# A decode block on one core: one 160 KB block of Down's weights loaded in the middle of the kernel by sixteen small loads instead of near the end by one

## The chip, the cores and the metric

The kernel runs on one core of a Trainium2 chip. The metric is the device time of one execution in microseconds (us). It was run three times for the table below, and one more execution was recorded by the profiler.

## What is computed

One token passes through an attention block over a cached context and then through a gated feed-forward block. Cut to what matters:

```python
mod = (silu(c) @ w_mod).reshape(1, 6, 1, 640)          # shifts, scales, gates
h = layernorm(x) * (1 + ca) + sa
q = h @ wq                                             # 32 heads of 128
p = softmax(q @ k_cache.T * 128**-0.5)                 # 16384 positions per head
x = x + ga * ((p @ v_cache) @ wo)
h = layernorm(x) * (1 + cb) + sb
x = x + gb * ((silu(h @ w_gate) * (h @ w_up)) @ w_down)   # 640 -> 1728 -> 640
```

All tensors are bf16. The K and V caches are 134 MB each, so nearly all of the 290 MB that is read is cache. `w_down` (called Down here) has 1728 rows of 640 values, 1280 bytes a row.

## The kernel before, in words

**Pairs of heads.** The 32 heads are taken in 16 pairs, p = 0 to 15. For each pair the kernel loads 8 MB of K (`load_k`, L487) and 8 MB of V (`load_v`, L493), each as 128 rows of 64 KB, one row per SBUF partition. K goes into one of two slots of the tile `kring`, V into the single tile `vbuf`; only the last V goes into a `kring` slot. VectorE multiplies K by q in place and folds the products in halves (L543, L548, L553; for the first and the last pair L559 and L565). TensorE finishes the sums (L533, L573), the maximum and the exponentials follow (L578 to L590), and TensorE multiplies the weights with V (`pv`, L499). The order of one round is `load_k(p + 1)`, `step(p)`, `load_v(p)` (L610 to L616).

**Who may start when.** The instructions are listed by hand and sent to the engines in that order; each waits for the operations that it names. All large loads are issued by SyncE (SP) on one queue, in program order. A K load waits until the sums of the pair that had its slot are done (L488); a V load waits until `pv` of the pair before is done (L494). TensorE, VectorE and ScalarE run the middle pairs in hardware loops; SP's list is written out in full.

**The end.** After the last K there follow on SP's queue, in this order: the last V, two pieces of `wo` (L628), gate and up weights (L638 and L640), and Down in five pieces (L642 to L648): three blocks of 512 rows with four rows per partition (640 KB each), one block of 128 rows with one row per partition (rows 1536 to 1663, 160 KB), and the last 64 rows cut in halves (80 KB). The five pieces are the entries of `DOWN` (L225). The weights go into the other `kring` slot and so wait for the last pair's sums (L637).

**Down's matmuls.** L743 to L757 walk through `DOWN` in the same order. A block with four rows per partition is 16 matmuls, the block with one row per partition is 4, the last piece is 4. Each block waits for its own load. After the first block a small matmul and a VectorE step (L759, L761) prepare the last piece. L763 and L764 then scale and add, and two small stores write the 640 results.

Of the kernel before, what the change touches and what calls it, by code (L numbers as in the profile page):

```python
# [6 lines left out]
BF16 = mybir.dt.bfloat16  # L7
# [30 lines left out]
class _Plan:  # L38
# [38 lines left out]
    def op(self, eng, fn, deps=(), name="", chan=None):  # L77
        o = _Op(eng, fn, list(deps), name, len(self.ops), self.loop.get(eng), chan)
        o.sig = chan is not None
        self.ops.append(o)  # L80
        return o

    def dma(self, out_ap, in_ap, key, deps=(), name="", eng="sp", noncontig=False):
        nc = self.nc

        def fn(e, out_ap=out_ap, in_ap=in_ap, noncontig=noncontig):
            if noncontig:
                with nc.allow_non_contiguous_dma(reason="tiny vector layout change"):
                    return e.dma_start(out_ap, in_ap)
            return e.dma_start(out_ap, in_ap)  # L90

        return self.op(eng, fn, deps, name, chan=self.dma_chan(key))
# [116 lines left out]
def build(nc, A_x, A_k, A_v, A_wq, A_wo, B_wg, B_wu, B_wd, c_in, w_mod, out):  # L209
    H, S, Dh = A_k.shape[1], A_k.shape[2], A_k.shape[3]  # L210
    D = A_x.shape[2]
# [3 lines left out]
    NP = H // 2  # L215
# [6 lines left out]

    BLOCKS = [(0, 4, 0), (512, 4, 4), (1024, 4, 8), (1536, 1, 12)]

    DOWN = [(0, 0, 4), (1, 0, 4), (2, 0, 4), (3, 0, 1), (None, 0, 0)]  # L225
    FCH = NF + 1
    QW = 32
    QR = 16
    RW = D // 4
# [3 lines left out]
    with es:  # L233
        plan = _Plan(nc, es)
        op, dma = plan.op, plan.dma
        POOL, ACT, DVE, PE = "pool", "act", "dve", "pe"

        def sb(name, shape, dtype):
            return es.enter_context(nc.sbuf_tensor(name, list(shape), dtype))
# [12 lines left out]
        wd_v = kb[:, wd0:wd0 + NF * D].rearrange("p (k n) -> p k n", k=NF)  # L252
# [47 lines left out]
        rg = sb("rg", [128, FCH], F32)  # L300
        sg = sb("sg", [128, FCH], F32)
        gu_col = sb("gu_col", [128, FCH], BF16)
        gu_half = sb("gu_half", [128, 2], BF16)
        even = sb("even", [128, 2], F32)
        twice = sb("twice", [128, 64, 2], BF16)
# [114 lines left out]
        def wide(col):  # L420
            return col.broadcast_to([col.shape[0], 32])
# [38 lines left out]
        for g in range(H // 4):  # L460
            b = g % 2
# [25 lines left out]
        def load_k(p):  # L487
            deps = [o_R[p - 2]] if p >= 2 else ([o_mod[1]] if p == 1 else [])  # L488
            cuts = KCUT if p == 0 else [0, T2]
            d_k[p] = [dma(kring[:, p % 2, a:b], k_src(p)[:, a:b], ("k", p % 2, c), deps=deps, name="dma_k%d_%d" % (p, c))  # L490
                      for c, (a, b) in enumerate(zip(cuts, cuts[1:]))]

        def load_v(p):  # L493
            deps = [o_R[NP - 2]] if p == NP - 1 else [o_pv[p - 1]] if p >= 1 else [o_q[-1]]  # L494
            cuts = VCUT if p == NP - 1 else [0, T2]
            d_v[p] = [dma(v_at(p)[:, a:b, :], v_src(p)[:, a:b, :], ("v", p == NP - 1, c), deps=deps, name="dma_v%d_%d" % (p, c))
                      for c, (a, b) in enumerate(zip(cuts, cuts[1:]))]
# [100 lines left out]
        def step(p):  # L598
            reduce_mm(p, 0, score(p, 0, before(p)))
            pv(p - 1)  # L600
            o_R[p] = reduce_mm(p, 1, score(p, 1))
            diag(p - 1)
# [7 lines left out]
        for p in range(1, NP - 1):  # L610
            plan.in_loop(("pe",), "pairs", p - 1, NLOOP)
            if p >= FIRST:
                plan.in_loop(("act", "dve"), "pairs", (p - FIRST) // 2, (NP - 1 - FIRST) // 2)
            load_k(p + 1)
            step(p)
            load_v(p)  # L616
        plan.out_of_loop(("pe", "act", "dve"))


# [20 lines left out]
        d_wu = dma(wu_v, wu_src, "wu", deps=wdeps, name="dma_wu")  # L640
        d_wd = []
        for i, (b, r0, r1) in enumerate(DOWN):  # L642
            if b is None:
                dst, src = wt_v, B_wd[NF * 128:F, :].rearrange("q (h n) -> (q h) n", h=2)
            else:
                f0, n, j0 = BLOCKS[b]
                dst, src = wd_v[:, j0 + r0:j0 + r1, :], B_wd[f0:f0 + 128 * n, :].rearrange("(p r) n -> p r n", r=n)[:, r0:r1, :]
            d_wd.append(dma(dst, src, ("wd", i), deps=wdeps, name="dma_wd%d" % i))  # L648
# [93 lines left out]
        o_gum = op(DVE, lambda e: e.tensor_tensor(out=gu_col[:], in0=u_ps[:, 0:FCH], in1=sg[:], op=ALU.mult), deps=[o_sg, o_u], name="gu")  # L742
        for i, (b, r0, r1) in enumerate(DOWN):  # L743

            if b is None:
                work = [(gu_half[:, r // 2:r // 2 + 1], wt_v[:, RW * (r % 2):RW * (r % 2) + RW], r) for r in range(4)]
            else:
                j0 = BLOCKS[b][2]
                work = [(gu_col[:, j:j + 1], wd_v[:, j, RW * r:RW * r + RW], r) for j in range(j0 + r0, j0 + r1) for r in range(4)]

            def f_down(e, i=i, work=work):
                last = None
                for at, (col, rows, r) in enumerate(work):
                    last = e.matmul(f_ps[32 * r:32 * r + 32, 0:RW], lhsT=wide(col), rhs=rows, start=(i == 0 and at < 4),  # L754
                                    stop=(i == len(DOWN) - 1 and at >= len(work) - 4), tile_position=(0, 32 * r))
                return last
            prev = op(PE, f_down, deps=[o_gum if b is not None else o_guh, d_wd[i], o_nb[PL]], name="down%d" % i)  # L757
            if i == 0:
                o_tw = op(PE, lambda e: e.matmul(attn_ps[:, 8:9], lhsT=twice[64:128].rearrange("p q h -> p (q h)"), rhs=gu_col[64:128, NF:FCH], start=True, stop=True),  # L759
                          deps=[o_gum, o_twice, o_abf], name="twice_gu")  # L760
                o_guh = op(DVE, lambda e: e.tensor_tensor(out=gu_half[:], in0=attn_ps[:, 8:9].broadcast_to([128, 2]), in1=even[:], op=ALU.mult),  # L761
                           deps=[o_tw, o_even], name="gu_half")
# [10 lines left out]
def bass_adaLN_cond__gqa_block_cached__swiglu_ffn__decode_kernel(  # L773
    nc: bass.Bass,
    A_x: bass.AP,
    A_k_cache: bass.AP,
    A_v_cache: bass.AP,
    A_wq: bass.AP,
    A_wo: bass.AP,
    B_x: bass.AP,  # L780
    B_w_gate: bass.AP,
    B_w_up: bass.AP,
    B_w_down: bass.AP,
    c: bass.AP,
    w_mod: bass.AP,
    out: bass.AP,
):
    build(nc, A_x, A_k_cache, A_v_cache, A_wq, A_wo, B_w_gate, B_w_up, B_w_down, c, w_mod, out)
# [28 lines left out]
```

## Time and profile before

| what | value |
|---|---|
| time, median of 3 runs (lowest to highest) | 679.35 us (679.03 to 679.57) |
| profiled execution, its own time | 679.08 us |
| profiled execution, its span on the core | 677.8 us |
| mean granted TensorE clock | 0.590 |
| read from memory | 290.47 MB, 429 GB/s over the span |

The profiler's span runs from the first to the last instruction on the core; the execution's own time holds 1.28 us more around it. A load has three moments in the profile: its issue on SP, the time its packets take on the 16 DMA engines, and its landing, when all of its parts have counted up the semaphore. A load waits in its queue behind the loads issued before it, so the time from issue to landing is mostly time in line.

### The profile page before, as it was taken

The page shows a single profiled execution, that of the slowest core. Times are in us where ns is not written, and L with a number is a line of the kernel's source. Part 1 is how long each engine was busy: PE and PEld are TensorE (multiplying, and loading weights), DVE is VectorE, ACT ScalarE, POOL GpSimd, SP SyncE. Part 2 cuts the span into 40 slices and gives each one's busy share as a digit, 9 for nine tenths or more (in the row PEclk, how much of TensorE's full clock was granted, in tenths as well). Part 3 has the DMA queues.
Part 4 walks back from the last instruction along what each step waited for, and adds up shares of the span by engine and source line. Part 5 has one row for each costly group of instructions (what it writes and reads, how often), then busy time and mean ns, then how long its engine had stood idle before and what let it go on. Part 6 is the DMA issues. An engine that isn't in the chain of part 4 may idle for free.

```text
span 677.8 us, 5368 instructions
## 1 busy us (share of the span) xinstructions
PE 365.1 (54%) x2052; PEld 143.7 (21%) x2053; DVE 513.6 (76%) x186; ACT 46.4 (7%) x146; POOL 0.7 (0%) x6
## 2 busy tenths in 40 slices
PE   2510475755728274654818375572818465481677
PEld 1100122221312122221302122121212222130236
DVE  2189997959596896959597795959699695959812
ACT  1110000100000000000000000000000000000010
POOL 0000000000000000000000000000000000000000
PEclk9765565655657565565757555575756556575665
DMA  9999999999999999999999999999999999999997
GB/s 375 441 461 433 433 433 430 433 430 433 433 430 433 433 433 433 433 433 433 433 433 433 433 433 433 433 433 433 433 433 437 433 433 437 433 433 433 433 400 312
DMA packets 6355, 290.58 MB, mean 429 GB/s; under 512 B 714, under 2 KB 972, under 8 KB 1484
## 3 DMA queue, kind: packets, MB, share of 16 engines
q1 hardware_dynamic: 6340, 290.48, 99.3%
q8 instruction: 5, 0.08, 0.0%
q14 instruction: 2, 0.02, 0.0%
q10 hardware_dynamic: 8, 0.00, 0.0%
HBM read 290.47 MB, written 0.00 MB: 429 GB/s over the span
## 4 chain that ended last, share of the span: by engine, by line
DMA 45%; DVE 30%; issue 13%; PE 11%; ACT 0%; DVEq 0%; SPq 0%
DMA kring<-in_A_k_cache_dram 45%; DVE kring L543 10%; PE psb L533 7%; DVE kring L548 6%; DVE kring L559 5%; DVE kring L565 5%; DVE kring L553 3%; PE psb L507 1%; PE psb L712 1%; PE psb L675 1%; PE psb L573 1%; PE psb L687 0%; PE psb L754 0%; DVE pm L578 0%; DVE nb L586 0%
## 5 line engine op out<-in xcount | busy, mean ns | idle before, releaser
L543 DVE TENSOR_TENSOR kring<-kring,qbc 128x16384 bf16<-128x16384 bf16 x28 | 243.3, 8688 | 96.3 <-DMA kring<-in_A_k_cache_dram 96.3
L533 PE MATMUL psb<-kring,ident 128*128 x448 | 197.5, 607 | 119.0 <-DVE kring L553 119.0
L548 DVE TENSOR_TENSOR kring<-kring 128x8192 bf16<-128x8192 bf16 x28 | 123.8, 4420 | 0.5
L533 PEld LDWEIGHTS psb<-kring,ident 128*128 128x128 bf16 x448 | 53.8, 120 | 246.9 <-issue 246.0
L507 PE MATMUL psb<-vbuf,PZ 128*8 128x512 bf16 x960 | 83.1, 521 | 0.0
L582 PE MATMUL psb<-d,bd_f 128*128 128x64 f32 x32 | 11.0, 446 | 118.7 <-ACT d L580 118.7
L553 DVE TENSOR_TENSOR kring<-kring 128x4096 bf16<-128x4096 bf16 x28 | 64.0, 2287 | 0.5
L559 DVE TENSOR_TENSOR kring<-kring,qbc 128x16384 bf16<-128x16384 bf16 x4 | 34.8, 8688 | 23.4 <-DMA kring<-in_A_k_cache_dram 23.4
L507 PEld LDWEIGHTS psb<-vbuf,PZ 128*8 128x8 bf16 x960 | 26.3, 109 | 61.3 <-issue 52.8
L573 PE MATMUL psb<-kring,ident 128*128 128x128 bf16 (+1 forms) x48 | 14.3, 464 | 45.3 <-DVE kring L565 45.3
L582 PEld LDWEIGHTS psb<-d,bd_f 128*128 128x128 f32 x32 | 8.0, 312 | 121.2 <-DVE pm L578 111.6
L565 DVE TENSOR_TENSOR kring<-kring 128x8192 bf16<-128x8192 bf16 (+2 forms) x12 | 31.7, 2645 | 0.3
L522 PEld LDWEIGHTS psb<-sel,acc_sb 128*128 128x128 f32 x128 | 28.5, 310 | 8.4 <-issue 4.3
L522 PE MATMUL psb<-sel,acc_sb 128*128 128x2 f32 x128 | 25.6, 322 | 1.4 <-ACT acc_sb L513 1.4
L513 ACT ACTIVATE acc_sb<-psb 128x512 f32<-128x512 f32 x16 | 9.6, 597 | 212.8 <-PE psb L507 212.8
L590 ACT ACTIVATE PZ<-psb,nb 64x256 bf16<-64x256 f32 x32 | 15.0, 468 | 64.8 <-DVE nb L586 64.6
L573 PEld LDWEIGHTS psb<-kring,ident 128*128 128x128 bf16 x48 | 5.6, 122 | 52.9 <-DVE kring L565 46.1
L580 ACT ACTIVATE d<-negid,pm 128x64 f32<-128x64 f32 x16 | 5.6, 348 | 155.3 <-DVE pm L578 155.3
L466 PE MATMUL psb<-vbuf,h_col 128*128 128x512 bf16 x39 | 9.8, 415 | 8.3 <-DMA vbuf<-in_A_wq_dram 8.3
L526 ACT ACTIVATE OT_sb<-psb 128x2 f32 (+1 forms) x16 | 2.8, 172 | 150.9 <-PE psb L522 150.9
L578 DVE TENSOR_REDUCE pm<-psb 128x1 f32<-128x256 f32 x16 | 6.7, 418 | 3.7 <-PE psb L573 3.7
L466 PEld LDWEIGHTS psb<-vbuf,h_col 128*128 128x128 bf16 x40 | 3.9, 106 | 14.5 <-DMA vbuf<-in_A_wq_dram 8.8
(105 smaller groups left out, 81.1 us busy)
## 6 DMA issues: line engine op xcount, KB each, us to landing
kring<-in_A_k_cache_dram SPq DMA_DIRECT2D x2, 4096.0 KB, 40.1
vbuf<-in_A_wq_dram SPq DMA_DIRECT2D x1, 5120.0 KB, 25.6
kring<-in_w_mod_dram SPq DMA_DIRECT2D x1, 4800.0 KB, 14.0
vbuf<-in_A_wo_dram SPq DMA_DIRECT2D x1, 4480.0 KB, 22.8
kring<-in_B_w_gate_dram SPq DMA_DIRECT2D x1, 2160.0 KB, 18.7
kring<-in_B_w_up_dram SPq DMA_DIRECT2D x1, 2160.0 KB, 23.5
kring<-in_B_w_down_dram SPq DMA_DIRECT2D x3, 640.0 KB, 25.1
vbuf<-in_A_wo_dram SPq DMA_DIRECT2D x1, 640.0 KB, 24.0
```

The source lines that it names most:

```text
L466: last = e.matmul(q_ps[b][:, 0:512], lhsT=h_col[:, k:k + 1].broadcast_to([128, 128]), rhs=wq_v[:, k, g * 512:(g + 1) * 512], start=(k == 0 ...
L507: last = e.matmul(acc_ps[32 * s:32 * s + 8, :], lhsT=PZ[:, j, :], rhs=v_at(p)[:, 4 * j:4 * j + 4, :].rearrange("p t d -> p (t d)"), start= ...
L522: last = e.matmul(OT_ps[:, 0:2], lhsT=acc_sb[:, 128 * i:128 * (i + 1)], rhs=sel[:, i:8:4], start=(i == 0), stop=(i == 3))
L533: last = e.matmul(S_ps[:, 0:T2], lhsT=ident[:], rhs=kring[:, bass.ds(plan.slot(p), 1), :, d].rearrange("p o t -> p (o t)"), start=(d == 0) ...
L543: return e.tensor_tensor(out=kv4, in0=kv4, in1=q4, op=ALU.mult)
L548: o_f = op(DVE, lambda e: e.tensor_tensor(out=kv4[:, :, 0], in0=kv4[:, :, 0], in1=kv4[:, :, 1], op=ALU.add), deps=[o_m], name="fold%d_%d" ...
L553: return op(DVE, lambda e: e.tensor_tensor(out=lo[:, :, 0:QR], in0=lo[:, :, 0:QR], in1=lo[:, :, QR:QW], op=ALU.add), deps=[o_f], name="fol ...
L559: o = op(DVE, lambda e: e.tensor_tensor(out=kv, in0=kv, in1=qbc[:, p, :].unsqueeze(1).broadcast_to([128, KCUT[c + 1] - KCUT[c], 128]), op= ...
L565: o = op(DVE, lambda e, w=w: e.tensor_tensor(out=kv[:, :, 0:w], in0=kv[:, :, 0:w], in1=kv[:, :, w:2 * w], op=ALU.add), deps=[o], name="fol ...
L573: last = e.matmul(S_ps[:, a:b], lhsT=ident[:], rhs=kring[:, p % 2, a:b, d], start=(d == 0), stop=(d == 15))
L582: o_mx[p] = op(PE, lambda e: e.matmul(mx_ps[:, 0:64], lhsT=bd_f[:], rhs=d2[:], start=True, stop=True), deps=[o_d2, o_bd1, o_bd2, o_nb[p - ...
L590: o_exp[p] = op(ACT, lambda e, half=half, ps=ps: e.activation(out=PZ[ps, :, 4 * half:4 * half + 4], in_=S_ps[ps, 0:T2].rearrange("p (c i) ...
```

## The change

The block with one row per partition gets a tile of its own, `wt`. Its load is cut into sixteen loads of 15, 14, 13, 12, 11, 10, 9, 8, 8, 7, 6, 5, 4, 3, 2 and 1 rows. They are issued by SP in round p = 8, after `load_v(8)` and before `load_k(10)`, without a wait, and count on one semaphore. The load of this block at the end is gone. Its four matmuls now stand second in Down's order, between the first and the second block of four rows per partition, and read `wt`. The other engines' lists have the same instructions as before, apart from this place in TensorE's.

```diff
-    DOWN = [(0, 0, 4), (1, 0, 4), (2, 0, 4), (3, 0, 1), (None, 0, 0)]
+    DOWN = [(0, 0, 4), (3, 0, 1), (1, 0, 4), (2, 0, 4), (None, 0, 0)]
+    EARLY = [15, 14, 13, 12, 11, 10, 9, 8, 8, 7, 6, 5, 4, 3, 2, 1]
...
+        wt = sb("wt", [128, D], BF16)
         gu_half = sb("gu_half", [128, 2], BF16)
...
             step(p)
             load_v(p)
+            if p == NP // 2:
+                at = 0
+                for n in EARLY:
+                    d_wt = dma(wt[at:at + n, :], B_wd[12 * 128 + at:12 * 128 + at + n, :], "wt", name="dma_wt%d" % at)
+                    at += n
+                assert at == 128
...
         for i, (b, r0, r1) in enumerate(DOWN):
+            if b == 3:
+                d_wd.append(d_wt)
+                continue
             if b is None:
...
-                work = [(gu_col[:, j:j + 1], wd_v[:, j, RW * r:RW * r + RW], r) for j in range(j0 + r0, j0 + r1) for r in range(4)]
+                work = [(gu_col[:, j:j + 1], (wt if b == 3 else wd_v[:, j])[:, RW * r:RW * r + RW], r) for j in range(j0 + r0, j0 + r1) for r in range(4)]
```

## The prediction

> **What bounds the kernel now.** I read the page's slices first, then the chain of waits, then the end of the kernel in the timeline. The page:
>
> ```profile
> span 677.8 us, 5368 instructions
> DMA  9999999999999999999999999999999999999997
> GB/s 375 441 461 433 433 433 430 433 430 433 433 430 433 433 433 433 433 433 433 433 433 433 433 433 433 433 433 433 433 433 437 433 433 437 433 433 433 433 400 312
> DMA 45%; DVE 30%; issue 13%; PE 11%; ACT 0%; DVEq 0%; SPq 0%
> ```
>
> The 16 DMA engines are busy in every slice and move 430 to 437 GB/s from the fourth slice to the 38th. Only the last slice is not full. The queue never runs dry, so whatever is put into it in the middle pushes everything behind it back. VectorE, next on the chain, does wait in the middle; this row is from the list of VectorE's waits between 100 and 610 us:
>
> ```profile
> DVE kring L543 <- DMA kring<-in_A_k_cache_dram: 96.3, 13, 8.3
> ```
>
> It waited for K in all 13 pairs there. So up to the last K's landing the DMA stream sets the time. What follows is told by the chain from there on (start, length, what):
>
> ```profile
> 569.99 38.73 DMA kring<-in_A_k_cache_dram
> 608.75 8.69 DVE kring L559
> ...
> 673.29 0.18 DVE gu_col L742
> 673.52 0.73 PE psb L754 x16
> 674.25 0.12 PE psb L759
> 674.36 1.49 PE psb L754 x22
> 675.87 0.34 DVE qbc L763
> 676.23 0.24 DVE o_row L764
> ```
>
> From 608.75 us to the end no DMA stands on the chain: 69 us of engine work follow on one another. The time is therefore the landing of the last K plus this engine work, as long as every later load comes before it is wanted. The last ones are close. Here are Down's last three pieces: their issues, two to a row (so 648.40, 648.88 and, 0.475 us on, 649.35), and their times to landing, and then TensorE's work on them:
>
> ```profile
> 648.40 0.91 SPq L90 DMA_DIRECT2D kring<-in_B_w_down_dram  x2
> 648.88 0.91 SPq L90 DMA_DIRECT2D kring<-in_B_w_down_dram  x2
> ```
>
> ```profile
> kring<-in_B_w_down_dram SPq DMA_DIRECT2D x1, 640.0 KB, 26.2
> kring<-in_B_w_down_dram SPq DMA_DIRECT2D x1, 160.0 KB, 26.2
> ...
> kring<-in_B_w_down_dram SPq DMA_DIRECT2D x1, 80.0 KB, 25.9
> ```
>
> ```profile
> 674.29 1.39 PE L754 MATMUL psb<-kring,gu_col 128*32 128x160 bf16 x36
> 675.34 0.15 PEld L754 LDWEIGHTS psb<-kring,gu_half 128*32 128x32 bf16 x4
> 675.47 0.35 PE L754 MATMUL psb<-kring,gu_half 128*32 128x160 bf16 x4
> ```
>
> Issue plus time to landing gives 674.60 us for the third 640 KB block, 675.08 for the 160 KB block and 675.25 for the 80 KB piece. The 36 matmuls are nine groups of four; with 0.35 us for the last, 1.39 us makes eight steps of 0.13. The third block's group (the fifth) starts at 674.81 with its weights loading one step before, at 674.68; the 160 KB block's (the ninth) weights load at 675.20; the last piece's at 675.34. Each load lands some 0.1 us ahead, and the steps run on into the last piece without a hole. The end of the DMA stream and the end of the engine work meet, but TensorE waits for none of the three.
>
> **The change, part by part.**
>
> *What goes at the end.* The 160 KB load leaves the queue's end. Between 674.60 and 675.08 it took 0.48 us there. The 80 KB piece lands 0.48 us earlier against the rest. As TensorE does not wait for it, that is worth nothing here: 0, and at most 0.48 us (0.07%) if in the timed executions the loads come some tenths later than in this one. I take 0.
>
> *TensorE's order.* The four matmuls move one block ahead. Their number stays; the blocks behind them are wanted one step of 0.13 us later, so the third block's margin grows from 0.08 to 0.21 us. The wait for the 160 KB block becomes a wait for a load of 280 us before: nothing waits. 0.
>
> *SP's queue.* The sixteen issues stand between V of pair 8 and K of pair 10. The timeline of SP, and their times to landing:
>
> ```profile
> 366.31 0.33 SPq L90 DMA_DIRECT2D vbuf<-in_A_v_cache_dram  x1
> 376.35 0.33 SPq L90 DMA_DIRECT2D kring<-in_A_k_cache_dram  x1
> ```
>
> ```profile
> vbuf<-in_A_v_cache_dram SPq DMA_DIRECT2D x1, 29.6
> kring<-in_A_k_cache_dram SPq DMA_DIRECT2D x1, 38.9
> ```
>
> Issues in a row start 0.475 us apart at the end of the kernel (648.40 to 648.88), so sixteen take 7.6 us and end at 374.3. SP then waits as before for the sums of pair 8, until 376.35: 2.1 us are left. If an issue were twice as dear, K of pair 10 would be issued at 381.8, while V of pair 8 keeps the engines busy until 366.31 + 29.6 = 395.9. The cover is 14 us even then. 0.
>
> *The sixteen loads' own time.* This is the term that counts. They carry 128 rows of 1280 bytes. As one load, 128 rows are 8 on each of 16 engines and took 0.48 us with their completions: 0.06 us a row. A lone row's cost in mid-stream shows in the load of x, in a window of 0.1 us, and the whole of ScalarE's queue on the page:
>
> ```profile
> q10 hardware_dynamic: 1, 0.00, 3.4%
> ```
>
> ```profile
> q10 hardware_dynamic: 8, 0.00, 0.0%
> ```
>
> 3.4% of 16 engines in 0.1 us is 0.054 us for its one packet. The queue's eight packets are two loads of one row and a store of two rows with one completion per row: a load of n rows, n under 16, uses n engines. So an engine gets between 0 and 16 of the rows, one per load that it takes part in, and is pushed back by 0 to 16 × 0.06 = 0.96 us; on average by 0.48.
>
> [...] No view here names a DMA engine.
>
> *Which engine matters.* K counts as landed when its slowest engine is done, and the sixteen are not abreast. The windows at the end, when nothing more is queued, and the page's count of code loads:
>
> ```profile
> 673.00:673.40 0.40, 0.18 (x6) 0.10 (x4) 0.11 (x1) 0.00 (x0) 0.00 (x0) 0.50 1.07 364
> 673.40:674.00 0.60, 0.48 (x16) 0.41 (x16) 0.06 (x1) 0.00 (x0) 0.00 (x0) 0.50 0.40 150
> 674.00:674.40 0.40, 0.40 (x15) 0.21 (x9) 0.00 (x1) 0.00 (x0) 0.00 (x0) 0.50 0.28 98
> 674.40:675.30 0.90, 0.90 (x32) 0.90 (x32) 0.16 (x1) 0.00 (x0) 0.00 (x0) 0.50 0.07 23
> ```
>
> ```profile
> q8 instruction: 5, 0.08, 0.0%
> ```
>
> The DMA share (the last column but one) falls from 1.07 through 0.40 and 0.28 to 0.07: from 673.4 us on the engines drop out one after another, the last at 675.25, a spread of some 1.8 us. Packets of code, 16 KB each and put into single engines' streams, are one cause that the page shows. An engine that is ahead by a microsecond can carry up to 16 rows for nothing; the slowest pays 0.06 us for each row it gets. If it gets none, the price is 0. If it gets 16, 0.96. Nothing in the profile says which engine is slowest, so I take the middle, 8 rows and 0.48 us. The engines behind it by a few tenths can take over as the slowest, which keeps the price off 0. This delay reaches the end whole: the last K lands 0.48 us later and 69 us of engine work start from it.
>
> **Sum.** Against the profiled execution: 677.8 span + 0.48 = 678.3, and with the 1.28 us around it 679.6 (now 679.08). The three runs' median is 0.27 us above the profiled execution, so 679.8 us, 0.07% slower. Bounds of this case: 679.35 + 0 and 679.35 + 0.96, or 679.3 to 680.3. A measurement of this kernel tells some 0.2%, 1.4 us, from no change, and the whole case lies within that.
>
> **The rivals.**
>
> *Rival 1, slower: each small load holds its engine until its row has been written and counted.* Then the price of a row isn't 0.06 us. The last wait of the kernel bounds it from above:
>
> ```profile
> SPq L768 <- DMA out_dram<-o_row: 1.0, 1, 1.0
> ```
>
> A lone small store took 1.0 us from issue to landing, with all its latencies. A nearer bound is the 80 KB piece, eight rows and one completion per engine, that landed 0.17 us after the load before it. At 0.17 us per small load, an engine that takes part in all sixteen is pushed back 2.7 us and one that takes part in eight 1.4. The slowest engine decides: from eight loads on it the kernel is slower by over 0.2%, up to 682.1. Against it: eight rows of data are in those 0.17 us, so the completion alone must be less. [...] I give this rival 0.11.
>
> *Rival 2, slower: SP is stopped by the number of loads in the queue.* With K of pair 9 and V of pair 8 ahead, the sixteenth is the 18th load under way. Before, the most shows at the end:
>
> ```profile
> 635.22 0.80 SPq L90 DMA_DIRECT2D vbuf<-in_A_wo_dram  x2
> 646.92 2.86 SPq L90 DMA_DIRECT2D kring<-in_B_w_down_dram  x5
> ```
>
> ```profile
> vbuf<-in_A_wo_dram SPq DMA_DIRECT2D x1, 4480.0 KB, 22.8
> ```
>
> wo lands at 658.0, so nine loads (two of wo, gate, up, five of Down) were under way at 649.35, and the last four issues kept their pace. If there is a limit between 9 and 17, SP stands until V of pair 8 has landed at 395.9, issues the rest (up to 9 × 0.475 us) and only then K of pair 10, with idle DMA engines and up to the lone store's 1.0 us before data flow. That is 1.0 to 5.3 us, 680.4 to 684.7. Nothing in the profile speaks for such a limit. 0.05.
>
> *Rival 3, a small gain: the end of the DMA stream counts after all.* If the timed executions have TensorE waiting for the last two pieces, and the slowest engine gets few rows, the time falls by up to 0.48 us, to 678.9. The margins of 0.1 us speak for it, the even pace of the matmuls against it. 0.12. A gain of over 0.2% would need 1.4 us, and no wait of that size hangs on the block.
>
> *The forecast case* has the remaining 0.72.
>
> **How the numbers follow.** Forecast 679.8. The range starts at rival 3's end, 678.9, and ends at 681.0, which takes in the forecast case with the runs' own scatter of 0.3 us and the lower half of rival 1; rival 2 and the rest of rival 1 stay out, about 0.1. Slower by over 0.2%: nearly all of rival 2 (0.05) and two thirds of rival 1 (0.08), 0.13. Faster by over 0.2%: 0.03 for what I don't see. Within 0.2%: 0.84.
>
> **What would show it.** Right: the chain of the profile after is the same and the last K's landing (608.75) moves to 608.8 to 609.7, with the engine work behind it again 69 us; K of pair 10 is still issued when pair 8's sums are done; the sixteen issues take some 7.6 us; the DMA slices stay full in mid-kernel; the 80 KB piece lands some 0.5 us further ahead of its matmuls. Rival 1: the K behind the small loads lands over 1.4 us later than 415.2 and the delay stays. Rival 2: a SP issue of several us near 370 and a slice of lower DMA share near 396. Rival 3: a last K no later, and a shorter end. What would make the forecast wrong is a slowest engine that gets no rows, or code packets that fall on other engines than before: the spread of 1.8 us comes from where they fall, and the change lengthens SP's code by 15 loads.

## The result, and the profile after

| | before | after |
|---|---|---|
| median (lowest to highest), 20 runs each | 679.23 us (679.01 to 679.57) | 680.63 us (680.15 to 680.85) |
| ratio, 95% interval | | 1.0019 [1.0013, 1.0025] |
| profiled execution: own time, span | 679.08, 677.8 us | 680.65, 679.4 us |
| mean granted TensorE clock | 0.590 | 0.595 |

The kernel is 1.40 us slower, 0.2%. The forecast was 0.5 us. The page of the kernel after:

```profile
span 679.4 us, 5383 instructions
GB/s 379 436 460 432 432 432 429 432 429 436 432 433 432 432 432 432 432 436 432 432 432 436 432 411 432 436 436 432 432 432 432 436 432 432 432 436 432 432 408 301
DMA 49%; DVE 30%; issue 13%; PE 8%; SPq 0%; DVEq 0%
```

One slice in mid-kernel stands out: the 24th, from 391 to 408 us, moved 411 GB/s where its neighbours have 432. Before, no slice from the fourth to the 38th was under 430. The sixteen loads fall into that slice. 21 GB/s over 17 us are 0.36 MB, or 0.8 us of the stream. The page counts the small rows among what the slice moved, so most of this loss is not the moving of their bytes.

The chain of waits of the kernel after (start, length, what), from the last K on:

```profile
571.86 38.73 DMA kring<-in_A_k_cache_dram
610.62 8.69 DVE kring L561
...
650.44 26.03 DMA kring<-in_B_w_down_dram
676.51 0.89 PE psb L765 x18
677.42 0.34 DVE qbc L774
677.78 0.24 DVE o_row L775
```

The last K is in use at 610.62 instead of 608.75: 1.87 us later. At the end the chain has a new link. TensorE waits for Down's third 640 KB block, which lands at 676.47 (674.60 before, 1.87 us later too). The engine work before it did not take its old length; the windows from the last K on, first of the kernel before, then of the kernel after (the last three columns are the TensorE clock, the DMA share and GB/s):

```profile
610.00:649.00 39.00, 15.52 (x109) 7.51 (x108) 32.85 (x12) 3.82 (x13) 0.00 (x0) 0.54 0.98 423
649.00:673.50 24.50, 20.36 (x294) 13.90 (x294) 4.29 (x22) 2.54 (x11) 0.00 (x0) 0.57 0.99 415
```

```profile
610.00:649.00 39.00, 16.06 (x116) 8.73 (x116) 33.88 (x11) 2.76 (x9) 0.00 (x0) 0.59 1.00 431
649.00:673.50 24.50, 18.24 (x277) 13.23 (x278) 4.35 (x22) 3.60 (x14) 0.00 (x0) 0.64 0.98 416
```

The granted clock was 0.64 instead of 0.57 in the second window. From the last K to Down's first matmul the work took 63.97 us (610.62 to 674.59) instead of 64.77 (608.75 to 673.52). Of these 0.8 us, 0.5 were lost again behind Down's first matmul (3.43 us to the end of the last step, 2.95 before), where TensorE now waits for the third block. So the span's account reads: 1.87 later K, some 0.3 us won at the end, 1.6 us in all (677.8 to 679.4).

SP's timeline of the kernel after:

```profile
366.41 0.33 SPq L90 DMA_DIRECT2D vbuf<-in_A_v_cache_dram  x1
366.79 5.73 SPq L90 DMA_DIRECT2D wt<-in_B_w_down_dram  x16
376.36 0.36 SPq L90 DMA_DIRECT2D kring<-in_A_k_cache_dram  x1
```

Sixteen issues took 5.7 us without a stop, and K of pair 10 was issued when it was before. The delay arises behind the issue, in the DMA engines.

Two readings below come from the trace's own records. **Landings**: each large load's sixteen parts count up its semaphore one by one, so a load has a mean and a slowest part (the sixteen small loads counted one part a row, 128 in all). K of pair 10 landed 1.42 us later in the mean and 1.87 at its slowest, and every later load kept that. **Packets**: the records give start and length of each row moved, and by joining ends to starts they can be laid out on sixteen engines. A 64 KB cache row takes 2.42 us undisturbed. At 392 to 400 us in the kernel after, all sixteen engines had cache rows of 2.6 to 3.5 us, also the one that carried none of the small rows: its cache row took 3.04 us, and it fell 0.67 us back. The engine that ended last carried 11 small rows, 0.7 us, and two of its cache rows took 2.82 and 3.39 us, 1.4 us more than undisturbed. As it had been 0.2 us ahead of the slowest engine, 1.87 of these 2.1 us show in K.

### The profile page after: what moved, and what is told of

The parts are those of the page before. It is cut to its first block, busy times and chain, and to the rows that moved or that the text cites. A ratio compares the mean times of both kernels' runs of the same rounds, so it can differ in the third digit from the quotient of the medians.

```text
span 679.4 us, 5383 instructions
## 1 busy us (share of the span) xinstructions
PE 359.6 (53%) x2052; PEld 143.0 (21%) x2053; DVE 513.5 (76%) x186; ACT 46.4 (7%) x146; POOL 0.7 (0%) x6
## 4 chain that ended last, share of the span: by engine, by line
DMA 49%; DVE 30%; issue 13%; PE 8%; SPq 0%; DVEq 0%
DMA kring<-in_A_k_cache_dram 45%; DVE kring L545 10%; PE psb L535 7%; DVE kring L550 6%; DVE kring L561 5%; DVE kring L567 5%; DMA kring<-in_B_w_down_dram 4%; DVE kring L555 3%; PE psb L575 1%; SPq L90 0%; DVE pm L580 0%; DVE nb L588 0%; PE psb L765 0%; DVEq L191 0%; DVEq L545 0%
## 5 line engine op out<-in xcount | busy, mean ns | idle before, releaser
L509 PE MATMUL psb<-vbuf,PZ 128*8 128x512 bf16 x960 | 79.0, 501 | 0.0
```

The lines of the kernel that those rows point to most:

```text
L509: last = e.matmul(acc_ps[32 * s:32 * s + 8, :], lhsT=PZ[:, j, :], rhs=v_at(p)[:, 4 * j:4 * j + 4, :].rearrange("p t d -> p (t d)"), start= ...
```

## The experiments

All times stand against the kernel before on the same chip (679.28 for e1 to e4, 679.22 for e5 to e8, 679.36 for e9 to e11, one run of 678.90 for e12). Diffs are against the kernel after unless said otherwise. The letters in the expectations are theories as they stood when each kernel ran. The first profile row of each shows the start of VectorE's work on the last K (608.75 before, 610.62 after). That start holds what its one profiled execution was off already ahead of the early loads: by the landings 0.27 us late in e2, 0.12 in e3, 0.2 in e4, 0.09 in e5, 0.08 in e7, 0.40 in e11, and 0.14 early in e6 (slowest part). Without this, the loads themselves added 1.85 us in the changed kernel, 0.44 in e1, 2.49, 2.82 and 2.2 in e2 to e4, 1.12, 1.22 and 2.7 in e5 to e7, 0.45 in e8 and 1.25 in e11.

### e1: one load instead of sixteen

```diff
-                at = 0
-                for n in EARLY:
-                    d_wt = dma(wt[at:at + n, :], ...)
-                    at += n
-                assert at == 128
+                d_wt = dma(wt[:], B_wd[12 * 128:13 * 128, :], "wt", name="dma_wt")
```

> The early block as one load of 128 rows in the same place; all else as in the changed kernel, where the last K lands 1.87 us later than before (610.62 against 608.75). Every engine has 8 rows and one completion. [...] Theory L (per load): each small load costs each of its engines some 0.15 us by itself; one load costs 0.15 beside the rows: 0.5 to 0.65, time 679.6 to 679.9. Theory M (memory): 16 engines read the same 160 KB of memory amid the stream, and that slows all of them; then the place matters and not the cut: 1.3 to 1.9 us as in the changed kernel, time 680.4 to 680.8.

```profile
GB/s 377 437 459 433 433 433 434 433 430 433 433 433 433 433 433 433 433 433 437 433 433 433 433 431 433 433 433 433 437 437 433 433 433 433 433 433 433 433 398 307
570.40 38.74 DMA kring<-in_A_k_cache_dram
609.16 8.69 DVE kring L561
```

679.46 us, ratio 1.0005 [0.9996, 1.0014]. The last K is 0.41 us later and the dip is gone (431). That is the 8 rows per engine at 0.05 us, as forecast for the middle. No cost of the early place, the tile or the new order of TensorE shows beside it; the cutting costs the rest. M fell, and L's 0.5 to 0.65 us nearly came.

### e2, e3, e4: other cuts into sixteen, and the same cut spread over rounds

```diff
+                for a in (0, 64):                                  # e2
+                    for j in (0, 1, 2, 3, 32, 33, 34, 35):
+                        at = a + j
+                        d_wt = dma(wt[at:at + 29:4, :], ...)
...
+                for at in range(0, 128, 8):                        # e3
+                    d_wt = dma(wt[at:at + 8, :], ...)
...
+            for i in {13: (12, 13), 14: (14, 15)}.get(p, (p - 1,)): # e4
+                at = sum(EARLY[:i])
+                d_wt = dma(wt[at:at + EARLY[i], :], ...)
```

> Sixteen loads of 8 rows in the same place, each writing every fourth partition (at, at+4, ... at+28). Eight engines carry 16 rows and 16 completions each, the other eight none. [...] Theory L (per load): 16 loads on an engine cost 16 x 0.15 = 2.4: last K 2.0 to 2.6 us later, time 680.7 to 681.4, and the same in the next run.

> [...] Loads, completions and rows per engine are those of the run before. [...] Theory L (per load): the same as the run before.

> The changed kernel's sixteen loads (15 down to 1 rows), one after each V of rounds 1 to 14 (two in rounds 13 and 14) in place of all in round 8. Rows and completions per engine are the changed kernel's. [...] Theory L (per load): as the changed kernel, 1.7 to 1.9 us, time 680.5 to 680.8.

```profile
611.51 8.69 DVE L561 TENSOR_TENSOR kring<-kring,qbc 128x16384 bf16<-128x16384 bf16 x1 [7.42 <-DMA kring<-in_A_k_cache_dram]
```

```profile
611.69 8.69 DVE L561 TENSOR_TENSOR kring<-kring,qbc 128x16384 bf16<-128x16384 bf16 x1 [7.41 <-DMA kring<-in_A_k_cache_dram]
```

```profile
611.13 8.69 DVE L561 TENSOR_TENSOR kring<-kring,qbc 128x16384 bf16<-128x16384 bf16 x1 [7.53 <-DMA kring<-in_A_k_cache_dram]
```

681.21 us (1.0028 [1.0017, 1.0038]), 681.28 (1.0028 [1.0019, 1.0038]) and 681.19 (1.0028 [1.0018, 1.0039]); the last K 2.76, 2.94 and 2.38 us later. If each load takes the same eight engines, as the sixteen one-row loads of e8 all took one, sixteen loads of 8 rows put all 128 on eight engines, 16 on each, 0.96 us at 0.06; nearly two thirds of the delay is again something else. 8 neighbouring partitions cost about the same as 8 partitions 4 apart (2.82 and 2.49 us by the loads themselves), and apart in time, in e4, the loads cost no less (2.2, and 1.85 in the kernel after). L, a price per load, seemed to hold in e2 and e3; for e4 it gave 1.7 to 1.9 us, too little.

### e5, e6, e7: fewer and larger loads

```diff
+                for at in range(0, 128, 16):                       # e5; e7: one of them in each round 1 to 8
+                    d_wt = dma(wt[at:at + 16, :], ...)
...
+                for at, n in ((0, 88), (88, 40)):                  # e6
```

> [...] New theory R (relative place): the sixteen engines stream 64 KB cache rows in a settled order relative to each other, and whatever pushes some of them and not the others makes all of them slower until they are settled again; what pushes all alike costs only its own time. R: as the single load, last K 0.4 to 0.6 us later than before, time 679.4 to 679.9. Theory L (per load, 0.15 us for each load an engine takes part in): 8 loads, 1.0 to 1.6 us, time 680.3 to 680.9. [...]

> The early block as two loads, of 88 and of 40 rows. [...] R: the uneven push slows all of them, last K 1.2 to 2.2 us later than before, time 680.2 to 681.2, although there are only two loads. L: the rows' own 0.72 us for the slowest loaded engine, which starts 0.1 ahead, and 2 x 0.15: 0.7 to 0.95 us, time 679.6 to 680.1.

> The eight loads of 16 rows, one per round in rounds 1 to 8. R: each pushes all engines alike, so spreading them costs nothing more: last K 0.4 to 0.6 us later than before, time 679.4 to 679.9, where sixteen uneven loads spread over the rounds made it 2.4 us. L: 1.0 to 1.6 us, time 680.3 to 680.9.

```profile
609.97 8.69 DVE L561 TENSOR_TENSOR kring<-kring,qbc 128x16384 bf16<-128x16384 bf16 x1 [7.43 <-DMA kring<-in_A_k_cache_dram]
```

```profile
609.83 8.69 DVE L561 TENSOR_TENSOR kring<-kring,qbc 128x16384 bf16<-128x16384 bf16 x1 [7.42 <-DMA kring<-in_A_k_cache_dram]
```

```profile
611.56 8.69 DVE L561 TENSOR_TENSOR kring<-kring,qbc 128x16384 bf16<-128x16384 bf16 x1 [7.43 <-DMA kring<-in_A_k_cache_dram]
```

680.29 us (1.0015 [1.0006, 1.0024]), 680.14 (1.0013 [1.0004, 1.0022]) and 681.55 (1.0032 [1.0020, 1.0044]). In e5 every engine has 8 rows, as in e1, but K is 1.21 us later instead of 0.41. In e6 the semaphore was counted up by 11 and by 10 engines: if the ten are among the eleven, ten have 12 rows, one has 8, five have none. 12 rows by themselves would be 0.72 us; K is 1.08 us later, and by the packets the engines without a row fell some 0.8 us back too. **Two** loads cost as much as eight, against L, which wanted 0.7 to 0.95 in e6 (for e5 it wanted 1.0 to 1.6, which came); one load in two pieces is enough to lose 0.7 us. R fell with e5 and e7. One load in each of eight rounds (e7) costs 2.8 us: the extra price came anew with each occasion.

### e8: sixteen loads of one row

Against the kernel before: the end stays as it was, and sixteen one-row loads come in round 8 into a tile that nothing reads.

```diff
+                for at in range(16):
+                    d_wt = dma(wt[at:at + 1, :], B_wd[12 * 128 + at:12 * 128 + at + 1, :], "wt", name="dma_wt%d" % at)
```

> The kernel before, whole, with sixteen loads of one row each added in round 8 into a tile that nothing reads (20 KB more to load). [...] The prediction's step: an engine that is ahead carries rows for nothing; its own push is 16 x 0.06 = 0.96 us, and the spread is 1.8, so last K no later than 0.2 us, time 679.2 to 679.6. L: 16 x 0.15 = 2.4 us on this engine, last K 0.6 to 2.4 us later depending on how far ahead it is, time 679.9 to 681.6. R: one engine out of sixteen moves against the others, which code packets also do: a smaller disturbance than an even half, last K 0.1 to 0.6 us later, time 679.3 to 679.9.

```profile
609.19 8.69 DVE L560 TENSOR_TENSOR kring<-kring,qbc 128x16384 bf16<-128x16384 bf16 x1 [7.41 <-DMA kring<-in_A_k_cache_dram]
```

679.43 us, 1.0003 [0.9994, 1.0012]; the last K 0.44 us later. By the packets all sixteen rows went through one engine. The first thirteen came 0.058 us apart, as priced. The last three took 0.13 to 0.18 us each, and the cache row behind them 3.39 us instead of 2.42, so this engine fell 2.1 us back: 0.13 us a load, where the prediction's price gives 0.96 us in all and L 2.4. It had been 1.7 us ahead of the slowest engine, and K shows only what was left over. The other fifteen engines fell back by 0.07 to 0.16 us. So these small loads held the engine that carried them for longer than their rows, and its lead hid most of it. A price per load on the engines that carry the loads is no account of e6, where engines without a row fell back as well.

### e9 and e10: six kinds of load in one run

Against the kernel before: trial loads of Down's rows into two tiles that nothing reads, each kind behind the V of another round. The K two pairs on then shows the delay.

```diff
+        near = [(16 * j, 16 * j + 16, 1, 16 * j, 1) for j in range(8)]   # first, end, step of partitions; first, step of rows
+        apart = [(j, j + 121, 8, j, 8) for j in range(8)]
+        near_apart = [(16 * j, 16 * j + 16, 1, j, 8) for j in range(8)]
+        apart_near = [(j, j + 121, 8, 16 * j, 1) for j in range(8)]
+        low = [(j, j + 29, 4, j, 4) for j in (0, 1, 2, 3, 32, 33, 34, 35)]
+        high = [(j, j + 29, 4, j, 4) for j in (64, 65, 66, 67, 96, 97, 98, 99)]
+        one112 = [(0, 112, 1, 0, 1)]
+        one128 = [(0, 128, 1, 0, 1)]
+        TRY = {2: near, 4: apart, 6: near_apart, 8: apart_near, 10: one112, 12: low}    # e9
+        TRY = {2: high, 4: one112, 6: apart, 8: near, 10: low, 12: one128}              # e10
...
+            for at, end, step_, src, gap in TRY.get(p, ()):
+                d_try.append(dma(trial[p // 2 % 2][at:end:step_, :], ...))
```

> The kernel before, whole, with trial loads of Down's rows added into two tiles that nothing reads, one kind per round, each after that round's V: round 2 eight loads of 16 neighbouring partitions from neighbouring rows (as in the run of eight loads); round 4 eight loads of 16 with partitions and rows eight apart; round 6 neighbouring partitions from rows eight apart; round 8 partitions eight apart from neighbouring rows; round 10 one load of 112; round 12 eight loads of 8 partitions four apart within 0 to 63. What each adds is read from the landing of the K behind it (K of pairs 4, 6, 8, 10, 12 and 14, before at 183.0, 260.4, 337.8, 415.2, 492.6 and 570.0 us). Pushes by the rows' own time: 0.48 for 128 rows, 0.42 for 112, up to 0.96 for the last kind on its eight engines. Theory H (home): a 128-row load gives each engine eight partitions, as the cache loads do; a row that an engine writes outside of its eight slows the whole stream. If the eight are neighbours, rounds 4 and 8 add 0.4 to 0.6, rounds 2 and 6 add 1.0 to 1.4, round 10 0.5 to 1.0. Theory M2 (memory): rows read side by side by several engines do it: rounds 2 and 8 add 1.0 to 1.4, rounds 4 and 6 add 0.4 to 0.6, round 10 0.4. Theory N (number): eight loads in a row cost it by their number: rounds 2, 4, 6 and 8 all 1.0 to 1.4, round 10 0.4.

> As the run before, other kinds in other rounds: round 2 eight loads of 8 partitions four apart within 64 to 127; round 4 one load of 112; round 6 the kind with partitions and rows eight apart; round 8 the kind with both neighbouring; round 10 eight loads of 8 partitions four apart within 0 to 63; round 12 one load of 128. Theory H with neighbours as the eight: round 6 0.4 to 0.6, round 8 1.0 to 1.4, round 4 0.5 to 1.0, round 12 0.4 to 0.5, rounds 2 and 10 alike and over their rows' own time. [...] Theory N: rounds 6 and 8 alike at 1.0 to 1.4, rounds 4 and 12 0.4 to 0.5.

VectorE's timeline, its start on the K behind rounds 2, 4, 6, 8, 10 and 12; the kernel before, then e10:

```profile
183.23 8.69 DVE L543 TENSOR_TENSOR kring<-kring,qbc 128x16384 bf16<-128x16384 bf16 x1 [7.17 <-DMA kring<-in_A_k_cache_dram]
260.63 8.69 DVE L543 TENSOR_TENSOR kring<-kring,qbc 128x16384 bf16<-128x16384 bf16 x1 [7.47 <-DMA kring<-in_A_k_cache_dram]
338.04 8.69 DVE L543 TENSOR_TENSOR kring<-kring,qbc 128x16384 bf16<-128x16384 bf16 x1 [7.47 <-DMA kring<-in_A_k_cache_dram]
415.45 8.69 DVE L543 TENSOR_TENSOR kring<-kring,qbc 128x16384 bf16<-128x16384 bf16 x1 [7.49 <-DMA kring<-in_A_k_cache_dram]
492.85 8.69 DVE L543 TENSOR_TENSOR kring<-kring,qbc 128x16384 bf16<-128x16384 bf16 x1 [7.48 <-DMA kring<-in_A_k_cache_dram]
570.25 8.69 DVE L543 TENSOR_TENSOR kring<-kring,qbc 128x16384 bf16<-128x16384 bf16 x1 [7.49 <-DMA kring<-in_A_k_cache_dram]
```

```profile
184.78 8.69 DVE L543 TENSOR_TENSOR kring<-kring,qbc 128x16384 bf16<-128x16384 bf16 x1 [8.40 <-DMA kring<-in_A_k_cache_dram]
263.20 8.69 DVE L543 TENSOR_TENSOR kring<-kring,qbc 128x16384 bf16<-128x16384 bf16 x1 [8.51 <-DMA kring<-in_A_k_cache_dram]
342.15 8.69 DVE L543 TENSOR_TENSOR kring<-kring,qbc 128x16384 bf16<-128x16384 bf16 x1 [9.03 <-ACT OT_sb L526]
421.34 8.69 DVE L543 TENSOR_TENSOR kring<-kring,qbc 128x16384 bf16<-128x16384 bf16 x1 [9.26 <-DMA kring<-in_A_k_cache_dram]
499.65 8.69 DVE L543 TENSOR_TENSOR kring<-kring,qbc 128x16384 bf16<-128x16384 bf16 x1 [8.40 <-DMA kring<-in_A_k_cache_dram]
577.47 8.69 DVE L543 TENSOR_TENSOR kring<-kring,qbc 128x16384 bf16<-128x16384 bf16 x1 [7.89 <-DMA kring<-in_A_k_cache_dram]
```

The distance grows from row to row: 1.55, 2.57, 4.11, 5.89, 6.80, 7.22 us. The last step, one load of all 128 rows, is 0.4; the second, one load of 112 rows, 1.0. From the landings, what each kind added (slowest part, and mean of the sixteen):

| kind | loads x rows | e9 slowest, mean | e10 slowest, mean |
|---|---|---|---|
| one128 | 1 x 128 | | 0.40, 0.39 |
| one112 | 1 x 112 | 1.14, 1.09 | 1.03, 0.98 |
| low: partitions 4 apart within 0 to 63 | 8 x 8 | 0.88, 0.38 | 0.90, 0.39 |
| high: the same within 64 to 127 | 8 x 8 | | 1.22, 0.85 |
| near: 16 neighbouring partitions | 8 x 16 | 0.98, 0.97 | 1.77, 1.54 |
| apart: partitions 8 apart | 8 x 16 | 1.48, 1.30 | 1.56, 1.25 |
| near_apart, apart_near (only rows or only partitions 8 apart) | 8 x 16 | 1.50, 1.21 and 1.55, 1.25 | |

(686.72 and 686.20 us, one run each.) A single load, at 112 rows instead of 128, costs over twice as much, though it moves less. And low and high differ only in the block's half, so in the partitions (and in which rows of Down are read): number and size of the loads and rows per engine are the same. So what sets low and high apart (0.38 to 0.39 and 0.85 us in the mean) is neither loads nor bytes but **which partitions are written**. Reading source rows side by side or eight apart makes no difference that clears the scatter: near itself cost 0.97 in one run and 1.54 in the other. None of the three theories of e9 came out whole: the kinds with eight loads of 16 all came to about 1 us or more, which is N's, but the one load of 112 did too, where N gave 0.4.

low has 64 rows, 8 on each of eight engines, so its rows' own time on these is 0.48 us and not the 0.96 that its expectation gives. It cost 0.88 to 0.90 at the slowest engine: the cheap kind is not free of a price beyond its rows either.

### e11: the changed kernel with partitions and rows 8 apart

```diff
+                for at in range(8):
+                    d_wt = dma(wt[at:at + 121:8, :], B_wd[12 * 128 + at:12 * 128 + at + 121:8, :], "wt", name="dma_wt%d" % at)
```

> The changed kernel with the early block as eight loads of 16 rows with partitions and rows eight apart, in round 8. Theories H and M2: last K 0.4 to 0.6 us later than before, time 679.4 to 679.8. Theory N: as eight loads of neighbours, 1.2 us later, time 680.2 to 680.4.

```profile
610.40 8.69 DVE L561 TENSOR_TENSOR kring<-kring,qbc 128x16384 bf16<-128x16384 bf16 x1 [7.42 <-DMA kring<-in_A_k_cache_dram]
```

680.43 us, 1.0017 [1.0008, 1.0026], K 1.65 us later, of which 0.40 were there ahead of the loads; the loads added 1.25. The first form of H, by which each engine's own partitions are eight neighbours, fell here, and M2 with it (both gave 0.4 to 0.6). N, with 1.2, came true in this run.

N cannot tell low from high, so what is left is H with other own partitions for each engine than eight neighbours. No view names an engine or the partitions that it writes, so which ones are an engine's own is the author's guess and not shown here. How the rows of the one load of 112 are dealt out no view shows either. What was measured is the order of the prices: in the mean 0.39 us for one128 and 0.38 for low, which has half as many rows, and 0.85 to 1.54 for all others.

### e12: low and high once more, and lone rows

The kernel before with other trial loads, in the same form. The names home0 and away0 go by the author's guess at H's own partitions:

```diff
+        near64 = [(8 * j, 8 * j + 8, 1, 8 * j, 1) for j in range(8)]
+        home0 = [(j, j + 1, 1, j, 1) for j in (0, 1, 2, 3, 32, 33, 34, 35)]
+        away0 = [(j, j + 1, 1, j, 1) for j in (64, 65, 66, 67, 96, 97, 98, 99)]
+        one64 = [(0, 64, 1, 0, 1)]
+        TRY = {2: low, 4: high, 6: near64, 8: home0, 10: away0, 12: one64}
```

> The kernel before with six kinds of trial loads, each behind the V of another round, into two tiles that nothing reads, so the outputs are computed as before. Round 2: low (eight loads, each of eight partitions 4 apart within partitions 0 to 63). Round 4: high (the same within 64 to 127). Round 6: eight loads of eight neighbouring partitions, all within 0 to 63. Round 8: eight loads of one row to partitions 0 to 3 and 32 to 35. Round 10: eight loads of one row to partitions 64 to 67 and 96 to 99. Round 12: one load of 64 rows to partitions 0 to 63. Of each kind I read how much later the K two pairs on lands than the one before it did (before: 183.0, 260.4, 337.8, 415.2, 492.6, 570.0 us). Theory H (a load costs its rows' own time where every engine writes the partitions that a load of 128 rows gives it, and slows the whole stream where engines write others): slowest engine plus 0.8 to 0.95 us for low, 1.1 to 1.3 for high, 1.0 to 1.4 for the neighbours, 0 to 0.5 for the one-row loads of round 8, 0.1 to 0.5 more than that for those of round 10, 0.4 to 0.9 for the one load of 64. Theory N (the price goes by the order of the kinds or by the number of loads): low now costs what high did in the run before or the two cost the same, the neighbours within 0 to 63 cost what low costs, and rounds 8 and 10 cost the same.

The same six starts of VectorE:

```profile
183.91 8.69 DVE L543 TENSOR_TENSOR kring<-kring,qbc 128x16384 bf16<-128x16384 bf16 x1 [7.92 <-DMA kring<-in_A_k_cache_dram]
262.97 8.69 DVE L543 TENSOR_TENSOR kring<-kring,qbc 128x16384 bf16<-128x16384 bf16 x1 [9.14 <-ACT OT_sb L526]
341.75 8.69 DVE L543 TENSOR_TENSOR kring<-kring,qbc 128x16384 bf16<-128x16384 bf16 x1 [8.85 <-DMA kring<-in_A_k_cache_dram]
419.17 8.69 DVE L543 TENSOR_TENSOR kring<-kring,qbc 128x16384 bf16<-128x16384 bf16 x1 [7.48 <-DMA kring<-in_A_k_cache_dram]
496.58 8.69 DVE L543 TENSOR_TENSOR kring<-kring,qbc 128x16384 bf16<-128x16384 bf16 x1 [7.50 <-DMA kring<-in_A_k_cache_dram]
574.91 8.69 DVE L543 TENSOR_TENSOR kring<-kring,qbc 128x16384 bf16<-128x16384 bf16 x1 [8.40 <-DMA kring<-in_A_k_cache_dram]
```

683.58 us, one run. Behind the kernel before by 0.68, 2.34, 3.71, 3.72, 3.73 and 4.66 us. From the landings and the packets (a cache row takes 2.42 us undisturbed):

| kind | expected by H, slowest | slowest, mean | cache rows beside it, on engines without trial rows |
|---|---|---|---|
| low | 0.8 to 0.95 | 0.74, 0.37 | none over 2.44 us |
| high | 1.1 to 1.3 | 1.66, 1.10 | 2.78 to 3.25, then 2.44 to 2.79 |
| near64 | 1.0 to 1.4 | 1.37, 0.77 | 2.61 to 2.80, then 2.55 to 2.60 |
| home0 | 0 to 0.5 | 0.01, 0.04 | none over 2.44 |
| away0 | 0.1 to 0.5 more | 0.01, 0.08 | 2.45, one of 2.71 |
| one64 | 0.4 to 0.9 | 0.93, 0.89 | (rows on all engines) |

low came first this time and is again the cheap one, and near64, which moves the same 64 rows to the same 64 partitions in eight loads of eight and differs in which of them go together in one load, costs twice its mean (0.77 us against 0.37): N fell on both, though rounds 8 and 10 cost the same at the slowest engine, as it said. The order of the kinds is H's. The last column shows where the price is paid. In low only the loaded engines' cache rows grew. In high and near64 the cache rows of engines that carried **nothing** of the trial took up to 0.8 us longer; each of these engines fell 0.7 to 0.9 us back in high and 0.38 in near64. The sizes missed H's bounds in four of six rows, on both sides. The real miss is away0, which H wanted dearer than home0 by 0.1 to 0.5 us: both cost 0.01 us at the slowest engine, and 0.08 and 0.04 in the mean. The engine with the eight rows fell 0.77 us back (0.73 in home0, where the rows' own time is 0.46), one other engine 0.29, the rest 0.03 or less. As none of these was the slowest, the landing of K shows 0.01. So in these two rounds rows on a single engine did not slow the whole stream, in whichever half of the partitions they were written; the 64 rows of high did.

## Why the prediction was right or wrong

**Right** in direction and range, the range with some luck. The change is small and slower, and 680.63 lies inside the range. But it lies above 680.3, the upper bound of the forecast case; it is inside because the range was widened for scatter and for the lower half of rival 1. And 1.40 us is 0.2%, just at the edge of "within 0.2%". Two of the signs named for the forecast did not come: the last K is at 610.62 and not at 608.8 to 609.7, and the chain has a new link. The sign named for rival 1 came: the K behind the small loads landed 1.87 us later (over 1.4), and the delay stayed.

**What bounds the kernel**: right up to the last K; the stream stayed full and the delay put in at 390 us was there, unchanged, at 608 us (slowest part 1.87 at both).

**Tail, TensorE's order, SP**: terms of nothing, as far as the runs can tell. e1 has the new end, e8 the old one; both have the last K 0.4 us later, and both are 0.2 us slower than before. SP's sixteen issues were cheaper than taken (0.36 us apart, not 0.475), and K of pair 10 kept its issue time. Rival 2 asked for a SP issue of several us, and there is none. Rival 3's gain at the end is not seen in this comparison of e1 with e8, but their intervals (0.6 us to either side) are as wide as the 0.48 us that it asked for.

**The sixteen loads' own time** is the step that failed, by its size: "So an engine gets between 0 and 16 of the rows, one per load that it takes part in, and is pushed back by 0 to 16 × 0.06 = 0.96 us". 0.06 us a row was right for the load of 128 rows from which it was taken (e1: 0.41 for 8). For lone rows it was right for the rows themselves and not for their engine: eight held it 0.73 us (home0), sixteen 2.1 (e8). And it leaves out the larger part: in some kinds of load the cache rows of the engines that carry none of the small rows stretch as well (in e12 2.78 to 3.25 us instead of 2.42 in high, none over 2.44 in low). The delay was 1.87 us where 0.48 was taken and 0.96 was the most. The rows from which the price came could not show it: they were those of a load over all 128 partitions and of a single lone row.

**The slowest engine**: the last one had 11 rows where I took 8; 0.2 us of the miss. It was not the slowest before but 0.2 us ahead of that one. That a lead hides a price held: in e8 a lead of 1.7 us left 0.44 of 2.1.

**It reaches the end whole**: nearly. "TensorE waits for none of the three" no longer held after: TensorE, at a granted clock of 0.64 instead of 0.57, caught up with the DMA stream, and the third block's landing set the end. Of the 0.8 us that the engine work had gained, 0.5 were lost again there.

**Rival 1** named the right sign and, by its formula (0.17 us times 11 loads), 1.9 us, but its mechanism is a part at most. Small loads did hold their own engine for longer than their rows (0.13 us a load in e8, 0.09 in home0). But two loads (e6) cost 1.08 us, and engines that carried none of the rows fell back as well: by 0.67 us in the kernel after, by 0.8 in e6. The right number would have come by luck. One load instead of sixteen was the cheaper form (e1: 679.46 us); overhead per load can be no more than that part of the time here.

**Left open**: why the whole stream slows; no run here shows a mechanism. Also open: how the 1.87 us divide between the price on the engines that carry small loads and the slowing of all of them; why e2, which is low and high in one round, has a mean of 1.63 us where the two by themselves add up to 1.22 to 1.49; and why near cost 0.97 once and 1.54 once.

No version was faster than the kernel before. Even the cheapest early load (e1) only moves 0.4 us from behind the last K to ahead of it, and before the last K the stream has no room.

## What to carry to other kernels

In a stream that is always full, price an added load first by its shape: here a load over all 128 partitions cost 0.4 us, no more than its rows' own time (0.48), and one of 112 rows 1.0 to 1.1. Cutting a load so that its pieces go to few engines does not by itself keep the cost on those engines (low did, 0.37 to 0.39 us in the mean, high did not, 0.85 to 1.10); look at the landings of the large loads around it, mean and slowest, to see whether the others were slowed. And take a price only from a row of the same shape as the thing priced; where there is none, the upper bound must not come from the same row.

## What was not expected of the hardware

- One load of 112 rows of 1280 bytes delayed the stream by 1.0 to 1.1 us, one of 64 rows by 0.9, one of 128 by 0.4.
- Engines that moved none of the small rows had 64 KB cache rows of up to 3.25 us instead of 2.42 beside them.
- A lag, once there, stayed: it was the same at the last K, 193 us on (mean 1.42, then 1.41).
- Where one load a round was put into eight rounds (e7), the cost was 2.8 us against 1.2 for the same loads in one round.
- SP issued the sixteen small loads of the kernel after every 0.36 us, those of e8 every 0.30.
- Sixteen loads of one row held the one engine that carried them for 2.1 us, of which the rows took 1.2 and a slower cache row behind them 1.0.
